# Gated linear attention feeding a SoLU block: the third token group's key work and scans placed before the second period

## The chip, the cores and the metric

The kernel runs on one core of a Trainium2 chip. The core has five engines that run side by side and wait for each other by semaphores: PE (matrix multiplication, with weight loads counted apart as PEld), DVE (VectorE), ACT (ScalarE), POOL (GpSimd) and SP (SyncE, which here only issues DMA transfers). Each engine works through its own instructions in the order in which the program gives them. The metric is the device time of one execution in microseconds (us).

## The reference

```python
# attention: batch 4, heads 8, sequence 768, head dimension 48, float32
state = np.zeros((B, H, D, D))
for t in range(S):
    state = alpha[:, :, t, :, None] * state + einsum('bhd,bhe->bhde', k[:, :, t], v[:, :, t])
    y[:, :, t] = einsum('bhd,bhde->bhe', q[:, :, t], state)
x = y.transpose(0, 2, 1, 3).reshape(B * S, H * D)      # 3072 tokens x 384

# SoLU block: w_in 384 x 1024, w_out 1024 x 384
h = x @ w_in
e = exp(h - max(h)); solu = h * e / sum(e)
ln = (solu - mean(solu)) / sqrt(var(solu) + 1e-06) * g_ln
out = ln @ w_out
```

## The kernel before, in words

**Tiling.** The 768 positions are cut into G = 6 groups of 128. A group holds the 128 positions of all four batches, 512 tokens, and is taken through two stages: attention (which makes `x`, 384 features by 512 tokens) and the SoLU block. In the SoLU block the 1024 hidden features are eight slices of 128. `up(g, f)` multiplies one slice (L366, six matmuls recorded for each, because float32 counts twice), takes its exponential on ACT (`e`, L380), the product h*e on DVE (`room`, L381) and its square on ACT (`u2`, L382). `running(g, f)` adds e on POOL and u2 on DVE into running sums (L397). `e` and `u2` have three buffers each, `h` has two PSUM banks. `down(n, half)` multiplies by w_out for one batch of a group (L477), and `finish(n)` scales and stores it (L495 to L511).

**Attention of a group.** The decay products over a group are made by scans on DVE. The steps, by the names that the plans use:

- `alpha` (alpha_T, L192, made for the group after the one in hand): alpha is transposed on DVE into `aT` and its range is checked on ACT (alpha_over, L197); then the alpha of one group further is loaded over it.
- `back` (scan_back, L211): three backward scans on DVE, `aT` to `hT`.
- `keys` (keys_T, L227, and keys, L231): the keys `kn` are transposed on DVE into `kT` (one transpose of 128x1024, one of 128x512), POOL multiplies them by `hT`, and the next group's keys are loaded over `kn`.
- `on2`, `on0`, `on1` (scan_on, L216): three forward scans on DVE, in place on `aT`; the one for part 2 first copies `fend` (L220). Each begins with `least` (L223) and a reciprocal (L224).
- `lasts`, `firsts`: the queries `qn` are transposed on DVE into `qe` and `qv`, and POOL multiplies them by `aT` (queries, L241); after `firsts` the next group's queries are loaded.
- `apart` (L235): ACT spreads `qe` over two parts of `qv`.
- `decay` (L246): POOL multiplies the state by the group's total decay.
- `keys_back` (L284): PE turns `kT` back, ACT copies the result to `kg`.
- `scores0`, `scores1` (L262): PE multiplies keys and queries for four heads at a time into four PSUM banks (a0 to a3); `masked0`, `masked1` (L276): DVE multiplies by the causal mask into `sT`. Both halves use the same four banks, and so do `keys_back`, the outputs y and the state update.
- `read0` to `read3` (L315): PE reads the old state into y. `values` (read_values, L323, then next_state, L333): PE adds sT times v to y, ACT copies y to `x` (L331), and PE makes the state update `kv`, which DVE adds to the state (L351).

**Order.** The schedule is written out by hand: the order of the calls is the order on every engine. Groups 0 and 1 have their attention in a straight-line part (L622 to L783), together with loading and unpacking the weights and all downs of group 0. Behind that comes the loop at L858, one *period* for each g = 1 to 5. Period g runs the eight ups of group g, the downs of group g - 1 (none in period 1, whose list `todo` is empty) and the attention of group g + 1 (up to g = 4). A plan says at which of the eight steps s each part of that attention comes: `head` before up(g, s), `behind` after it, `middle` after the running sums, and `tail` after the down of the step. Period 1 has the plan `first`, period 2 the plan `second`, later periods `usual`. Under `first` the backward scans of the next group (`back`) are not made; `second` makes them late, as `back_late` at its step 0.

**SP's queue.** All loads in the loop and the stores of finish (but for the last group) are issued by SP, in program order: a store waits for its scaled output on ACT, `load_v` for the state update that still reads the old v, loads of k and q for the DVE transposes of the old ones, a load of alpha for alpha_over.

Of the kernel before, what the change touches and what calls it, by code (L numbers as in the profile page):

```python
# [32 lines left out]
def fast_path(ctx, tc, q, k, v, alpha, moe_w_in, moe_w_out, moe_g_ln, out):  # L33
# [68 lines left out]
    kn = const.tile([P, H, TQ, D], FP, name="kn")  # L102
# [26 lines left out]
    def load(src, dst, g):  # L129
        t = slice(g * P, (g + 1) * P)  # L130
        for b in range(B):
            nc.sync.dma_start(
                out=dst[32 * b : 32 * b + 32].rearrange("t h u d -> t h (u d)"),
                in_=src[b, :, t, :].rearrange("h (t u) d -> t h (u d)", u=TQ),
            )
# [47 lines left out]
    def firsts(src, dst):  # L183
        nc.vector.transpose(out=dst.rearrange("p h (t u) -> p h u t", u=TQ), in_=src[:, :, :, 0:E0])  # L184

    def lasts(src, dst):
        nc.vector.transpose(
            out=dst.rearrange("p j (i t u) -> p u j i t", u=TQ, i=2),
            in_=src[:, :, :, E0:D].rearrange("p (j i) u d -> p u j i d", i=2),
        )  # L190

    def alpha_T(g):  # L192
        nc.gpsimd.memset(aT[:, :, 0:1], 0.0)
        firsts(an, aT[:, 0:H, 1:SW])
        lasts(an, aT[:, H:NB, 1:SW])
# [9 lines left out]
    def scan(out, data, start, flip):  # L205
        a, o, s = (x.rearrange("p j s -> p (j s)") for x in (data, out, start))
        if flip:
            a, o, s = a[:, ::-1], o[:, ::-1], s[:, ::-1]
        nc.vector.tensor_tensor_scan(out=o, data0=a, data1=s, initial=1.0, op0=ALU.mult, op1=ALU.add)  # L209

    def scan_back(g, i):  # L211

        part = slice(NP * i, NP * i + NP)
        scan(h4[:, part], aT[:, part], unit, True)

    def scan_on(g, i):  # L216
        part = slice(NP * i, NP * i + NP)
        s = seed[i % 2]
        if i == 2:
            nc.vector.tensor_copy(out=fend[:, g], in_=h4[:, :, 1])  # L220

        least = small.tile([P, NP, 1], FP, name="least")
        nc.vector.tensor_scalar(out=least, in0=h4[:, part, 1:2], scalar1=LEAST, scalar2=None, op0=ALU.max)  # L223
        nc.vector.reciprocal(out=s[:, :, 0:1], in_=least)  # L224
        scan(aT[:, part], aT[:, part], s, False)

    def keys_T(g):  # L227
        firsts(kn, kT[:, 0:H])
        lasts(kn, kT[:, H:NB])

    def keys(g):  # L231
        for part in (slice(0, H), slice(H, NB)):
            nc.gpsimd.tensor_tensor(out=kT[:, part], in0=kT[:, part], in1=hk[:, part], op=ALU.mult)  # L233
# [64 lines left out]
    def y_mm(b, a, r, row, lhsT, rhs, stop=False):  # L298
        begun = reading["begun"]
        nc.tensor.matmul(  # L300
            y_bank(b)[quarter(r), a], lhsT=lhsT, rhs=rhs, start=(b, r) not in begun, stop=stop,
            tile_position=(row, 32 * r), skip_group_check=True,
        )
        begun.add((b, r))
# [18 lines left out]
    def read_values(g, batches=range(B)):  # L323
        if 0 in batches:
            gr[g]["x"] = pair.tile([P, KC, B, P], FP, name="x")
        for b in batches:
            for n, (a, hs) in enumerate(parts):
                for r, (h, e) in enumerate(hs):
                    y_mm(b, a, r, 0, vn[:, b, h, e], sT[:, b, h], n == len(parts) - 1)
        for b in batches:  # L330
            nc.scalar.copy(out=gr[g]["x"][:, :, b], in_=reading["y"][b])  # L331

    def next_state(g):  # L333
        kv = banks("kv", [H, 64], 2)
        for j in range(NB):
            for b in range(B):
                if j < H:
                    o, e = kv[0][quarter(b), j], vn[:, b, j, 0:64]
                else:
                    i = 2 * (j - H)  # L340
                    o, e = kv[1][quarter(b), i : i + 2], vn[:, b, i : i + 2, 0:64]
                nc.tensor.matmul(  # L342
                    o, lhsT=kg[:, j, quarter(b)], rhs=e, start=True, stop=True, tile_position=(0, 32 * b),
                    skip_group_check=True,
                )
        for i in range(2):
            s = state[:, H * i : H * i + H, 0:64]
            if g == 0:
                nc.scalar.copy(out=s, in_=kv[i])
            else:  # L350
                nc.vector.tensor_tensor(out=s, in0=s, in1=kv[i], op=ALU.add)  # L351
# [426 lines left out]
    load(alpha, an, 3)  # L778
    for i in range(3):
        scan_back(2, i)  # L780
    read_values(1)
    next_state(1)
    finish(3)  # L783
# [3 lines left out]
    usual = dict(  # L787
        head={4: "keys_back", 5: "masked0", 6: "masked1"},
        behind={0: "v keys", 1: "on2 on0 on1", 2: "lasts firsts", 3: "apart", 5: "decay", 6: "alpha", 7: "back"},
        tail={4: "scores0", 5: "scores1", 6: "begin read0 read1", 7: "values"},  # L790
        middle={7: "read2 read3"},
    )
    first = dict(
        head={4: "keys_back", 6: "masked0", 7: "masked1"},
        behind={0: "v keys", 1: "on2 on0", 2: "on1 lasts", 3: "firsts", 4: "apart", 5: "decay", 7: "alpha"},
        tail={5: "scores0", 6: "scores1", 7: "begin read0 read1 read2 read3 values"},
        middle={},
    )
    second = dict(
        head={4: "keys_back", 6: "masked0", 7: "masked1"},  # L800
        behind={0: "back_late", 1: "v keys", 2: "on2 on0 on1", 3: "lasts firsts", 4: "apart", 5: "decay", 6: "alpha", 7: "back"},
        tail={5: "scores0", 6: "scores1", 7: "read2 read3 values"},
        middle={7: "begin read0 read1"},
    )

    def attend(a, what):

        more = a + 1 < G
        if what == "v":
            load_v(a)  # L810
        elif what == "keys":
            keys_T(a)
            keys(a)
            if more:
                load(k, kn, a + 1)
        elif what[:2] == "on":
            scan_on(a, int(what[2]))
        elif what == "lasts":
            lasts(qn, qe)
            queries(2)  # L820
        elif what == "firsts":
            firsts(qn, qv[:, 0:H])
            queries(0)
            queries(1)
            if more:
                load(q, qn, a + 1)
        elif what == "apart":
            apart()
        elif what == "decay":
            decay(a)  # L830
        elif what == "keys_back":
            keys_back(a)
        elif what[:6] == "scores":
            scores(a, int(what[6]))
        elif what[:6] == "masked":
            masked(int(what[6]))
        elif what == "alpha" and more:
            alpha_T(a + 1)
            alpha_over(a + 1)
            if a + 2 < G:  # L840
                load(alpha, an, a + 2)
        elif what == "back" and more:
            for i in range(3):
                scan_back(a + 1, i)
        elif what == "back_late":
            for i in range(3):
                scan_back(a, i)
        elif what == "begin":
            read_begin()
        elif what[:4] == "read":  # L850
            read_state(int(what[4]))
        elif what == "values":
            read_values(a)
            next_state(a)
# [2 lines left out]
    todo = []  # L857
    for g in range(1, G + 1):  # L858
        rise, att = g < G, g + 1 < G
        plan = {1: first, 2: second}.get(g, usual)  # L860

        def at(where, s):
            for what in plan[where].get(s, "").split() if att else ():
                attend(g + 1, what)

        after = None
        if not rise:
            break
        for s in range(FC):
            at("head", s)  # L870
            if rise:
                up(g, s)
            if after is not None:
                finish(after)
                after = None
            if s == 0 and g > 1:
                token_sums(g - 1)
            at("behind", s)
            for f in centres.get(s, ()) if g == 1 else ():
                centre(f)  # L880
            if rise and s:
                running(g, s)
            at("middle", s)
            if todo:
                n, half = todo.pop(0)
                down(n, half)
                if half:
                    after = n
            at("tail", s)
        if after is not None:  # L890
            finish(after)
        todo = [(n, half) for n in range(g * B, g * B + B) for half in range(2)]
# [493 lines left out]
```

## Time and profile before

| | |
|---|---|
| median of 14 runs | 405.13 us (401.61 to 408.27) |
| the profiled execution | 406.92 us; span of its core 405.1 us |
| mean granted clock of PE | 0.985 |
| busy: PE, DVE, ACT, POOL | 378.5, 255.8, 146.2, 117.6 us |
| up matmuls L366 | 288, 592 ns median of one |
| down matmuls L477 | 384, 491 ns mean of one |
| DVE backward scans L209, each | 1257 ns mean |
| DVE forward scans L209, each | 1387 ns mean |
| POOL key products L233 | 8, 1739 ns mean |
| first up matmul of periods 1 to 5, start | 117.97, 162.15, 220.81, 278.28, 335.75 us |
| k load, one of four issues of a group | 192 KB, 4.2 us to landing |

The profile is of one execution. The rows of the group table give, for one line of the program and one engine, the number of instructions, their busy time and the mean of one, and the time that the engine stood idle just before them with what ended it. In a timeline a row is one instruction, or a merged stretch of the same instruction ("x12"), with its start from the beginning of the span. "issue" as the cause of a pause means that the profile shows nothing that was waited for. The stretches between the starts in the table's row of the first up matmuls are the periods.

### The profile page before, as it was taken

The page shows a single profiled execution, that of the slowest core. Times are in us where ns is not written, and L with a number is a line of the kernel's source. Part 1 is how long each engine was busy: PE and PEld are TensorE (multiplying, and loading weights), DVE is VectorE, ACT ScalarE, POOL GpSimd, SP SyncE. Part 2 cuts the span into 40 slices and gives each one's busy share as a digit, 9 for nine tenths or more (in the row PEclk, how much of TensorE's full clock was granted, in tenths as well). Part 3 has the DMA queues.
Part 4 walks back from the last instruction along what each step waited for, and adds up shares of the span by engine and source line. Part 5 has one row for each costly group of instructions (what it writes and reads, how often), then busy time and mean ns, then how long its engine had stood idle before and what let it go on. Part 6 is the DMA issues. An engine that isn't in the chain of part 4 may idle for free. (4 is left out here: it accounts for less than half of the span.)

```text
span 405.1 us, 11119 instructions
## 1 busy us (share of the span) xinstructions
PE 378.5 (93%) x4929; PEld 229.4 (57%) x4929; DVE 255.8 (63%) x415; ACT 146.2 (36%) x253; POOL 117.6 (29%) x118
## 2 busy tenths in 40 slices
PE   8686999788988898999999999999999999999995
PEld 8673436356664357555557555567555675555552
DVE  1978789994929874699592795574875413444410
ACT  3535575553332525123351224243152122222100
POOL 5010000030005696074630438120466110333200
PEclk9998999998999899999999999999999999999999
DMA  9956969403319203632130833002400000000111
GB/s 186 196 159 171 227 196 194 97 19 80 79 48 170 60 22 83 79 98 47 52 100 4 134 69 92 2 23 41 59 19 21 23 3 21 15 15 11 40 40 47
DMA packets 86409, 30.82 MB, mean 76 GB/s; under 512 B 67912, under 2 KB 84560, under 8 KB 86352
## 3 DMA queue, kind: packets, MB, share of 16 engines
q1 hardware_dynamic: 85328, 29.11, 33.2%
q8 instruction: 40, 0.66, 0.7%
q10 hardware_dynamic: 1024, 0.92, 0.7%
q14 instruction: 17, 0.14, 0.1%
HBM read 25.30 MB, written 4.72 MB: 74 GB/s over the span
## 5 line engine op out<-in xcount | busy, mean ns | idle before, releaser
L366 PE MATMUL h<-x,w_in 128*128 128x512 f32 x288 | 135.4, 612 | 6.9 <-DVE g_col L596 4.2
L477 PE MATMUL o<-w_out,room 128*128 128x385 f32 x384 | 133.2, 491 | 1.1 <-DVE least L223 1.1
L477 PEld LDWEIGHTS o<-w_out,room 128*128 128x128 f32 x384 | 71.4, 190 | 57.2 <-issue 15.4
L366 PEld LDWEIGHTS h<-x,w_in 128*128 128x128 f32 x288 | 53.5, 192 | 67.6 <-issue 50.8
L381 DVE TENSOR_TENSOR room<-h,e 128x512 f32<-128x512 f32 x40 | 27.6, 690 | 56.7 <-ACT e L380 56.6
L508 POOL TENSOR_TENSOR r<-sums,mhalf 128x1 f32<-128x1 f32 x20 | 12.1, 607 | 172.2 <-DVE sums L500 172.1
L380 ACT ACTIVATE e<-h 128x512 f32<-128x512 f32 x40 | 23.9, 596 | 82.2 <-PE h L366 82.2
L397 POOL TENSOR_TENSOR p<-p,e 128x512 f32<-128x512 f32 x30 | 42.1, 1403 | 21.9 <-ACT e L380 21.7
L382 ACT ACTIVATE u<-room 128x512 f32<-128x512 f32 x40 | 25.2, 630 | 50.1 <-DVE room L381 50.1
L279 DVE TENSOR_TENSOR sT<-a,mask 128x512 f32<-128x512 f32 x44 | 27.3, 682 | 12.4 <-PE a L268 12.4
L268 PE MATMUL a<-qv,kT 32*128 32x128 f32 x704 | 26.2, 291 | 4.5 <-DVE qv L758 2.0
L268 PEld LDWEIGHTS a<-qv,kT 32*128 32x128 f32 x704 | 23.2, 197 | 11.5 <-issue 3.6
L397 DVE TENSOR_TENSOR p<-p,u 128x512 f32<-128x512 f32 x30 | 24.0, 800 | 7.0 <-ACT u L382 7.0
L209 DVE TENSOR_TENSOR_SCAN hT<-aT,unit 128x516 f32<-128x516 f32 x18 | 21.8, 1257 | 8.2 <-ACT aT L655 8.2
L209 DVE TENSOR_TENSOR_SCAN aT<-aT,seed 128x516 f32<-128x516 f32 x18 | 25.0, 1387 | 0.6
L351 DVE TENSOR_TENSOR state<-state,kv 128x512 f32<-128x512 f32 x10 | 6.9, 688 | 28.7 <-PE kv L342 28.7
L300 PE MATMUL y<-sT,vn 128*32 128x128 f32 x768 | 22.9, 274 | 1.4 <-issue 0.8
L331 ACT COPY x<-y 128x384 f32<-128x384 f32 x24 | 11.5, 479 | 31.6 <-PE y L300 31.6
L233 POOL TENSOR_TENSOR kT<-kT,hT 128x1024 f32<-128x1024 f32 (+1 forms) x8 | 13.7, 1739 | 31.5 <-DVE kT L184 31.5
L300 PEld LDWEIGHTS y<-sT,vn 128*32 128x32 f32 x768 | 20.8, 110 | 3.7 <-issue 2.8
L300 PE MATMUL y<-qv,state 32*32 32x128 f32 x1280 | 20.1, 278 | 2.0 <-issue 1.6
L300 PEld LDWEIGHTS y<-qv,state 32*32 32x32 f32 x1280 | 15.9, 103 | 9.5 <-issue 6.5
(140 smaller groups left out, 388.2 us busy)
## 6 DMA issues: line engine op xcount, KB each, us to landing
an<-in_alpha_dram SPq DMA_DIRECT2D x20, 192.0 KB, 4.2
out_dram<-o_sb SPq DMA_DIRECT2D x20, 192.0 KB, 1.9
room<-in_moe_w_out_dram SPq DMA_DIRECT2D x8, 384.0 KB, 3.7
kn<-in_k_dram SPq DMA_DIRECT2D x16, 192.0 KB, 4.2
qn<-in_q_dram SPq DMA_DIRECT2D x16, 192.0 KB, 3.5
vn<-in_v_dram SPq DMA_DIRECT2D x5, 512.0 KB, 5.7
room<-in_moe_w_in_dram SPq DMA_DIRECT2D x16, 128.0 KB, 4.0
kn<-in_k_dram SPq DMA_DIRECT2D x4, 384.0 KB, 5.8
```

The lines of the kernel that those rows point to most:

```text
L209: nc.vector.tensor_tensor_scan(out=o, data0=a, data1=s, initial=1.0, op0=ALU.mult, op1=ALU.add)
L233: nc.gpsimd.tensor_tensor(out=kT[:, part], in0=kT[:, part], in1=hk[:, part], op=ALU.mult)
L268: nc.tensor.matmul(a[b][:, i], lhsT=kT[quarter(b), kb], rhs=qv[quarter(b), qb], start=kb == h, stop=kb != h, tile_position=(32 * b, 0), sk ...
L279: nc.vector.tensor_tensor(out=sT[:, b, half * NP : half * NP + NP], in0=a[b], in1=mask[:, None, :].to_broadcast([P, NP, P]), op=ALU.mult,)
L300: nc.tensor.matmul(y_bank(b)[quarter(r), a], lhsT=lhsT, rhs=rhs, start=(b, r) not in begun, stop=stop, tile_position=(row, 32 * r), skip_g ...
L366: nc.tensor.matmul(h, lhsT=w_in[:, a, f * P : (f + 1) * P], rhs=d["x"][:, a].rearrange("p b t -> p (b t)"), start=(a == 0), stop=(a == KC ...
L380: nc.scalar.activation(out=e, in_=h, func=AF.Exp)
L381: nc.vector.tensor_tensor(out=u, in0=h, in1=e, op=ALU.mult)
L382: nc.scalar.activation(out=u2, in_=u, func=AF.Square)
L397: eng.tensor_tensor(out=p, in0=d[0][i] if f == 1 else p, in1=d[f][i], op=ALU.add)
L477: nc.tensor.matmul(d["o"][:, 0 : DM + 1], lhsT=u_of(g, f)[:, b * P : b * P + P], rhs=w_out[:, f], start=(f == 0), stop=(f == FC - 1), skip ...
L508: nc.gpsimd.tensor_tensor(out=r, in0=s[:, 3:4], in1=mhalf, op=ALU.pow)
```

## The change

In the straight-line part, after the backward scans of group 2, the keys of group 2 are transposed and multiplied, the load of group 3's keys is issued, and two of the three forward scans of group 2 are made. All this now comes ahead of `read_values(1)`, `next_state(1)` and `finish(3)` in program order. Period 1's plan loses these parts. Its remaining parts come a step earlier at several places, its state reads are split between steps 6 and 7, and it makes the backward scans of group 3 at step 7. The plan `second` and the late backward scans are taken out; period 2 runs under `usual`.

```diff
     load(alpha, an, 3)
     for i in range(3):
         scan_back(2, i)
+    keys_T(2)
+    keys(2)
+    load(k, kn, 3)
+    scan_on(2, 2)
+    scan_on(2, 0)
     read_values(1)
     next_state(1)
     finish(3)
...
     first = dict(
-        head={4: "keys_back", 6: "masked0", 7: "masked1"},
-        behind={0: "v keys", 1: "on2 on0", 2: "on1 lasts", 3: "firsts", 4: "apart", 5: "decay", 7: "alpha"},
-        tail={5: "scores0", 6: "scores1", 7: "begin read0 read1 read2 read3 values"},
-        middle={},
-    )
-    second = dict(
-        head={4: "keys_back", 6: "masked0", 7: "masked1"},
-        behind={0: "back_late", 1: "v keys", 2: "on2 on0 on1", 3: "lasts firsts", 4: "apart", 5: "decay", 6: "alpha", 7: "back"},
-        tail={5: "scores0", 6: "scores1", 7: "read2 read3 values"},
-        middle={7: "begin read0 read1"},
+        head={3: "keys_back", 5: "masked0", 6: "masked1"},
+        behind={0: "v", 1: "on1", 2: "lasts firsts", 3: "apart", 5: "decay", 7: "alpha back"},
+        tail={4: "scores0", 5: "scores1", 6: "begin read0 read1", 7: "values"},
+        middle={7: "read2 read3"},
     )
...
-        elif what == "back_late":
-            for i in range(3):
-                scan_back(a, i)
...
-        plan = {1: first, 2: second}.get(g, usual)
+        plan = first if g == 1 else usual
```

For comparison, the plan `usual`, which is not changed:

```python
head={4: "keys_back", 5: "masked0", 6: "masked1"},
behind={0: "v keys", 1: "on2 on0 on1", 2: "lasts firsts", 3: "apart", 5: "decay", 6: "alpha", 7: "back"},
tail={4: "scores0", 5: "scores1", 6: "begin read0 read1", 7: "values"},
middle={7: "read2 read3"},
```

## The prediction

> **What bounds the kernel now.** I read the page's busy shares first (PE 93%), then the chain that ended last (the last 0.8 us only, no use), then busy time by stretch. The stretches run from the first up matmul (L366) of one period to that of the next: "period g" is the pass of the L858 loop with that g. The columns after the length are busy time and count for PE, PEld, DVE, ACT, POOL, then the granted clock and the DMA share.
>
> ```profile
> core 0: us, PE busy (x) PEld busy (x) DVE busy (x) ACT busy (x) POOL busy (x), PEclk, DMA share, GB/s
> 110.70:117.20 6.50, 4.77 (x194) 4.35 (x190) 0.03 (x1) 1.92 (x4) 0.00 (x0) 1.00 0.33 79
> 118.00:162.10 44.10, 39.12 (x671) 23.76 (x668) 33.33 (x45) 17.81 (x30) 28.67 (x25) 0.96 0.39 78
> 162.10:220.80 58.70, 58.30 (x768) 35.04 (x764) 43.27 (x61) 19.15 (x32) 21.41 (x19) 1.00 0.31 66
> 220.80:278.30 57.50, 57.50 (x769) 34.54 (x765) 37.87 (x60) 19.94 (x33) 20.96 (x20) 1.00 0.28 57
> ```
>
> Period 3 (last row) already runs under the later plan and PE never pauses: 57.5 us is its own work. Period 2 does the same work in 58.7, so at most 1.2 us is to be had there. Period 1 is the loose one: it has no down matmuls, so its own work is 57.5 less period 3's eight downs (2.6 to 2.8 us each in PE's timeline, 21.3 together) and the token sums (0.6): 35.6 us. It takes 44.2. The other 8.6 us are waits and a slow clock. In the first row DVE and POOL stand still for 6.5 us just before it, while PE reads out group 1.
>
> Who holds PE in period 1: the waits there, then DVE's and PE's timelines (start, duration, instruction, idle before it).
>
> ```profile
> ACT u L382 <- DVE room L381: 13.7, 8, 5.7
> PEld h L366 <- DVE room L381: 4.4, 3, 2.9
> ```
> ```profile
> 117.22 0.69 DVE L351 TENSOR_TENSOR state<-state,kv 128x512 f32<-128x512 f32 x1 [6.49 <-PE kv L342]
> ...
> 122.09 2.04 DVE L184 STREAM_TRANSPOSE kT<-kn 128x1024 f32<-128x1024 f32 x1
> 123.97 1.10 DVE L187 STREAM_TRANSPOSE kT<-kn 128x512 f32<-128x512 f32 x1
> ...
> 125.50 0.99 DVE L220 COPY fend<-hT 128x12 f32<-128x12 f32 x1
> ...
> 126.81 1.88 DVE L209 TENSOR_TENSOR_SCAN aT<-aT,seed 128x516 f32<-128x516 f32 x1
> 128.61 1.18 DVE L223 TENSOR_SCALAR least<-hT 128x4 f32<-128x4 f32 x1
> ...
> 130.04 1.23 DVE L209 TENSOR_TENSOR_SCAN aT<-aT,seed 128x516 f32<-128x516 f32 x1
> ...
> 131.77 0.68 DVE L381 TENSOR_TENSOR room<-h,e 128x512 f32<-128x512 f32 x1
> ```
> ```profile
> 132.51 4.97 PE L366 MATMUL h<-x,w_in 128*128 128x512 f32 x7 [2.66 <-DVE room L381]
> ```
>
> The room product that frees an h bank (there are two) sits behind fend, two scans and a running sum, from 125.50 to 131.77, so PE stands for 2.66 us. The 0.99 us fend and 1.18 us least are small operations (0.16 each elsewhere) that ran late because POOL's key product and running sum lay beside them.
>
> **The change, ahead of period 1.** Moved to DVE after scan_back(2), which ends at 110.7: the key transposes (starts 122.09 to 124.90: 2.8 us), fend, least, reciprocal and scan for part 2 (125.50 to 128.61: 3.1, with POOL's delay in it), the same for part 0 (1.5; the second least's delay came from a running sum that isn't there). 7.4 us in a gap of 6.5. Place by place: transposes to 113.5; POOL's products 112.9 to 116.1 (their row: 3.3); fend to 115.1; scan 2 to 117.3; scan 0 to 118.8. Queued behind on DVE are the two state additions (were 117.22, now 118.75) and finish(3), each 1.3 us late. Nobody needs the new state before POOL's decay, 20 us on; kv's banks are next wanted by keys_back near 126. finish(3)'s ACT scaling delays the first exponential from 120.85 to 121.75, its room product from 121.5 to 122.4, and PE needs that only for up 2 at 123.1. Cost 0; without PE's two h banks it would be the 0.9.
> The k load of group 3 (four issues, 3.1 us on SP) now follows alpha's at about 113.6 and precedes finish(3)'s store and the v load, which wait for later things anyway; the v load moves by 0.9 us, and is wanted 25 us on. The q load goes 7 us earlier.
>
> **Period 1**, with the rows' durations, absolute times as before. DVE: room 1 at 124.3; scan 1 waits for POOL's first running sum (124.3 to 125.6) and ends 127.2; running 1; room 2 at 127.7 (it was 131.77); q transposes 128.3 to 131.3; running 2; room 3 at 131.7. PE: up 2 to 125.75, keys_back (1.3) to 127.05, up 3 to 129.6, up 4 to 132.2. No wait on room is left. What is late next is scores0: POOL's q products end 134.3, and apart on ACT, which comes after keys_back's copies (1.5), e3 and u2 3, ends at 134.35. PE waits 132.2 to 134.5: **2.3**. Scores0 to 136.5, masks 138.1 to 140.5 (running 4 holds DVE while POOL runs), up 5 has ended at 139.1: wait **1.45** before scores1, since both halves use the same four banks and no down stands between them. Then masks1 against read0: **0.4**. At the end ACT's alpha_over (3.35 from 152.1) delays the copies of y, whose banks kv needs: **0.8**. Sum 4.95 + 35.6 = 40.5 against 44.2: **-3.7**.
> The clock has to be added.
>
> ```profile
> 130.20:133.60 3.40, 1.09 (x3) 0.62 (x4) 3.33 (x6) 1.11 (x2) 0.00 (x0) 1.00 0.21 39
> 133.60:137.00 3.40, 3.40 (x6) 1.35 (x5) 3.40 (x5) 0.86 (x3) 1.92 (x2) 0.53 0.01 2
> ...
> 154.10:157.50 3.40, 1.84 (x84) 1.37 (x68) 2.12 (x3) 2.49 (x4) 3.40 (x4) 1.00 0.02 5
> ```
>
> A stretch of 3.4 us in which PE worked 1.09 is followed by one at half clock; one in which it worked 1.84 isn't. My 2.3 us wait leaves 1.1 if it falls in one such stretch, and more if it straddles two. At half clock the scores take 3.61 (the row at 92.61) and not 2.0, right on the path: 0 to **+1.6**. It lies at the edge, so I take +0.8.
> [...]
>
> **Period 2** gets the plan of period 3 (masks one step earlier, reads apart) and loses the three late scans at its start (3.5 us of DVE). It begins with the same state as period 3, the state additions about a microsecond later and the next room product another microsecond behind them: 57.5, **-1.2**. If the additions were later still, token_sums would hold PE; I bound that at +0.5.
>
> Sum: -3.7 + 0.8 - 1.2 = **-4.1**. The profiled execution took 406.92 (span 405.1), so 402.8 there. It is 1.8 above the median of the runs; from the median, 405.13 - 4.1 = **401.0**.
>
> **Rivals.**
> *Denser than I think.* POOL and DVE get in each other's way less, apart comes in time, and period 1 keeps only waits of about 0.8: 36.4, so -7.8 - 1.2 = -9.0: 396.1; halfway there, with only the 2.3 us wait shortened to 0.5 and no slow clock, -6.7: 398.4. For it: DVE has 7 us less work in this period. Against: scores now follow up 4 with no step in between, where before PE still waited at 139.7 and 140.8 with a step more.
> *The wait only moves.* The 2.3 us become 4 (q products behind running sums on POOL) and the clock drops fully: -4.1 + 1.7 + 0.8 = -1.6: 403.5, hardly to be told from no change. For it: POOL has the same 28.7 us less 3.3 in a shorter period, and apart must wait for both POOL and ACT.
> *Slower: the k load in front of PE's densest code.* PE already pauses for nothing that the profile shows, twice just there:
>
> ```profile
> 112.13 2.93 PE L300 MATMUL y<-sT,vn 128*32 128x128 f32 x99 [0.82 <-issue]
> ...
> 116.41 1.63 PE L342 MATMUL kv<-vn,kg 128*32 128x64 f32 x70 [0.90 <-issue]
> 158.00:160.00 2.00, 2.00 (x82) 2.00 (x75) 0.00 (x0) 1.21 (x3) 0.19 (x1) 1.00 0.80 200
> ```
>
> [...] If each pause grew to a k transfer's landing (4.2 us by the DMA table), it would cost 3.4 + 3.3 = 6.7, net +2.6: 407.7. It decides from 2.9 us a pause. Against: the last row, the same matmuls at DMA share 0.80 without a pause, and a 1.56 us pause at 156.31 with share 0.02.
> [...]
>
> **Chances.** Forecast (399.3 to 403.1) 0.52; denser 0.22; the wait only moves 0.18; slower 0.08. 0.5% is 2.0 us, about what a measurement can tell, so faster means under 403.1: 0.52 + 0.22 + 0.02 = 0.76; same 0.16; slower 0.08. The range runs from the middle of the denser case, 397, to just past the moved wait, 404.5.
>
> **What would show it.** Right: key transposes and two scans between 110.7 and 119, DVE idle there near zero; no wait of L366 on room over 1 us; period 1 near 40 to 42 us, with waits before both scores; period 2 at 57.5; pauses at 111 to 117 still under 1 us each. Wrong: period 1 starting over 1 us later (prelude step), a wait before scores0 over 4 us, or period 2 over 58.5.

## The result and the profile after

The changed kernel took 397.13 us (median of 10 runs, 396.46 to 402.1) against 404.83 us before (median of 47 runs, 401.61 to 408.49). The ratio of its runs to those of before is 0.9852, with a 95% interval of 0.9814 to 0.9889: about 6 us less, between 4.5 and 7.5. The ratio goes by the means of those runs that lie within 1.5% of the fastest of their kernel (here 398.65 us against 404.65, without five of the 47; in the experiments a run of 487 us of the kernel before and one of 966 us of the last version fall out by this too). The medians lie further apart, by 7.7 us, because the changed kernel's runs fall into two clumps, six at 396.5 to 397.2 us and four at 400.8 to 402.1: the median stands in the lower one, the mean between them. The profiled execution took 398.24 us (span 396.4).

Busy time by stretch of the changed kernel; columns as before: length, busy time of PE, PEld, DVE, ACT and POOL, granted clock, DMA share.

```profile
108.22:116.32 8.10, 6.72 (x212) 5.38 (x203) 7.96 (x10) 1.92 (x4) 3.35 (x2) 1.00 0.66 157
114.90:154.50 39.60, 38.34 (x671) 23.08 (x668) 30.63 (x41) 17.39 (x30) 24.08 (x23) 1.00 0.33 61
154.50:212.00 57.50, 57.50 (x769) 34.53 (x765) 38.72 (x60) 19.37 (x32) 20.39 (x19) 1.00 0.37 75
```

The first row is DVE's work that was put ahead of period 1; the gap of 6.5 us in which DVE did nothing is gone. Period 1 (second row) takes 39.6 us and not 44.2, with the clock at full speed throughout. Period 2 (third row) takes 57.5 and not 58.7; PE never pauses in it.

Who holds PE in period 1 now (all of PE's rows in the waits of that stretch), and PE's timeline at those places:

```profile
PE a L268 <- POOL qv L244: 0.4, 1, 0.4
PE a L268 <- ACT qv L237: 0.3, 1, 0.3
PE h L366 <- DVE room L381: 0.3, 1, 0.3
```
```profile
120.58 2.84 PE L366 MATMUL h<-x,w_in 128*128 128x512 f32 x6 [0.27 <-DVE room L381]
...
130.32 0.50 PE L268 MATMUL a<-qv,kT 32*128 32x128 f32 x8 [0.43 <-POOL qv L244]
131.15 2.01 PE L268 MATMUL a<-qv,kT 32*128 32x128 f32 x56 [0.33 <-ACT qv L237]
133.09 2.84 PE L366 MATMUL h<-x,w_in 128*128 128x512 f32 x6
135.86 3.62 PE L268 MATMUL a<-qv,kT 32*128 32x128 f32 x64
```

The 2.66 us wait for room is down to 0.27. The last row is a nearly hidden wait: 64 score matmuls take 2.07 us elsewhere and 3.62 here, because they stop between the first ones until the masks of the first half have freed the banks. No wait of PE's rows shows these 1.55 us; the whole list has 0.6 of them, at the weight loads (PEld).

DVE ahead of period 1:

```profile
108.22 2.06 DVE L184 STREAM_TRANSPOSE kT<-kn 128x1024 f32<-128x1024 f32 x1
110.09 1.25 DVE L187 STREAM_TRANSPOSE kT<-kn 128x512 f32<-128x512 f32 x1
111.08 1.57 DVE L220 COPY fend<-hT 128x12 f32<-128x12 f32 x1
...
112.98 1.88 DVE L209 TENSOR_TENSOR_SCAN aT<-aT,seed 128x516 f32<-128x516 f32 x1
...
115.17 1.23 DVE L209 TENSOR_TENSOR_SCAN aT<-aT,seed 128x516 f32<-128x516 f32 x1
116.32 1.26 DVE L351 TENSOR_TENSOR state<-state,kv 128x512 f32<-128x512 f32 x2
```

8.1 us from the first transpose to the state additions, which now follow without a gap; fend (1.57) and the first scan (1.88) lie beside POOL's key product (110.43 to 113.78) and again take longer than elsewhere (0.16 and 1.23).

### The profile page after: what moved, and what is told of

Its sections match the earlier page's. It is cut to its first block, busy times and chain, and to the rows that moved or that the text cites. A ratio compares the mean times of both kernels' runs of the same rounds, so it can differ in the third digit from the quotient of the medians.

```text
span 396.4 us, 11123 instructions
## 1 busy us (share of the span) xinstructions
PE 375.2 (95%) x4929; PEld 227.4 (57%) x4929; DVE 254.5 (64%) x415; ACT 146.1 (37%) x253; POOL 115.4 (29%) x118
## 5 line engine op out<-in xcount | busy, mean ns | idle before, releaser
L397 POOL TENSOR_TENSOR p<-p,e 128x512 f32<-128x512 f32 x30 | 41.0, 1365 | 24.7 <-ACT e L380 24.4
L397 DVE TENSOR_TENSOR p<-p,u 128x512 f32<-128x512 f32 x30 | 24.8, 827 | 8.6 <-ACT u L382 8.6
L268 PE MATMUL a<-qv,kT 32*128 32x128 f32 x704 | 25.0, 278 | 4.6 <-DVE qv L758 2.0
L268 PEld LDWEIGHTS a<-qv,kT 32*128 32x128 f32 x704 | 22.0, 186 | 11.8 <-DVE qv L758 2.8
L300 PE MATMUL y<-sT,vn 128*32 128x128 f32 x768 | 23.1, 274 | 1.3 <-issue 0.8
L300 PEld LDWEIGHTS y<-sT,vn 128*32 128x32 f32 x768 | 20.8, 110 | 4.2 <-issue 2.7
L300 PEld LDWEIGHTS y<-qv,state 32*32 32x32 f32 x1280 | 15.3, 103 | 7.6 <-issue 4.1
L300 PE MATMUL y<-qv,state 32*32 32x128 f32 x1280 | 19.0, 278 | 0.0
L201 ACT ACTIVATE sq<-an,mone 128x1536 uint8<-128x1536 f32 x12 | 18.8, 1570 | 0.2
```

Of the source, the lines that this page charges most:

```text
L201: nc.scalar.activation(out=sq, in_=x, func=AF.Relu, scale=sign, bias=mone, accum_out=over[:, g, i : i + 1])
L268: nc.tensor.matmul(a[b][:, i], lhsT=kT[quarter(b), kb], rhs=qv[quarter(b), qb], start=kb == h, stop=kb != h, tile_position=(32 * b, 0), sk ...
L300: nc.tensor.matmul(y_bank(b)[quarter(r), a], lhsT=lhsT, rhs=rhs, start=(b, r) not in begun, stop=stop, tile_position=(row, 32 * r), skip_g ...
L397: eng.tensor_tensor(out=p, in0=d[0][i] if f == 1 else p, in1=d[f][i], op=ALU.add)
```

## The experiments

The table gives, for each kernel, the length of periods 1 and 2 and of a *stretch* from the first state read of group 1 (the first 32x32 matmul of L300 after the scores of group 1) to the first up of period 3, all from one profiled execution. The stretch starts behind the half-clock stretches of the straight-line part; the two pauses at issue ahead of period 1 lie in it and still differ (1.2 to 2.0 us together without fillers). Times are medians; a ratio is to the kernel before on the same chip, with its 95% interval. The chips differ between the rows, so their times are compared by the ratios.

| kernel | period 1 | period 2 | stretch | time | ratio |
|---|---|---|---|---|---|
| before | 44.18 | 58.66 | 117.04 | 404.83 | |
| changed | 39.62 | 57.47 | 110.95 | 397.13 | 0.985 (0.981 to 0.989) |
| only the move | 39.17 | 58.87 | 112.19 | 400.35 | 0.990 (0.985 to 0.995) |
| only the plans | 44.73 | 57.47 | 116.48 | 402.17 | 0.998 (0.993 to 1.003) |
| old period 2 | 39.24 | 58.77 | 111.92 | 400.37 | 0.989 (0.983 to 0.996) |
| k load in period 1 | 39.09 | 57.48 | 110.59 | 399.32 | 0.986 (0.979 to 0.993) |
| keys alone ahead | 43.02 | 57.48 | 114.79 | 401.75 | 0.994 (0.990 to 0.998) |
| three scans ahead | 40.43 | 57.47 | 111.94 | 398.17 | 0.987 (0.982 to 0.992) |
| one filler | 39.71 | 57.48 | 111.27 | 400.22 | 0.990 (0.986 to 0.994) |
| two fillers | 42.59 | 57.73 | 113.41 | 400.71 | 0.990 (0.986 to 0.994) |
| before, two fillers | 47.03 | 60.04 | 119.92 | 407.66 | 1.007 (1.003 to 1.011) |
| second scores later | 43.47 | 57.48 | 114.66 | 401.69 | 0.994 (0.990 to 0.998) |
| two fillers, output banks | 40.58 | 57.50 | 111.21 | 399.21 | 0.987 (0.982 to 0.993) |
| output banks | 38.04 | 57.48 | 109.95 | 396.09 | 0.976 (0.970 to 0.983) |

### The move without the new steps, and the new steps without the move

```diff
-        head={3: "keys_back", 5: "masked0", 6: "masked1"},
-        behind={0: "v", 1: "on1", 2: "lasts firsts", 3: "apart", 5: "decay", 7: "alpha back"},
-        tail={4: "scores0", 5: "scores1", 6: "begin read0 read1", 7: "values"},
-        middle={7: "read2 read3"},
+        head={4: "keys_back", 6: "masked0", 7: "masked1"},
+        behind={0: "v", 2: "on1 lasts", 3: "firsts", 4: "apart", 5: "decay", 7: "alpha"},
+        tail={5: "scores0", 6: "scores1", 7: "begin read0 read1 read2 read3 values"},
+        middle={},
...
+    second = dict(...)      # as before, with back_late
```

> Only the move ahead of period 1: the period keeps the old steps for what is left in it, and period 2 its old plan with the late scans. Theory (the waits of up matmuls on room came from the key chain on DVE, and the move alone takes them away): no wait of L366 on room over 1 us, period 1 at 39 to 41 us against 44.2 before and 39.6 after the change, period 2 at 58.5 to 59; time 4 to 5 us under before. Rival (the earlier steps of the plan are what shortens period 1): period 1 at 42 to 44, time within 2 us of before.

PE in period 1 of this kernel has no wait for room, neither at up 2 nor at up 4:

```profile
118.40 10.57 PE L366 MATMUL h<-x,w_in 128*128 128x512 f32 x24
...
130.11 5.32 PE L366 MATMUL h<-x,w_in 128*128 128x512 f32 x12
```

Period 1 took 39.17 us and period 2 58.87, and the time is 4.0 us under before by the ratio: as the theory had it. The move alone does all that the change does for period 1.

```diff
-    keys_T(2)
-    keys(2)
-    load(k, kn, 3)
-    scan_on(2, 2)
-    scan_on(2, 0)
...
-        behind={0: "v", 1: "on1", ...},
+        behind={0: "v keys", 1: "on2 on0 on1", ...},
```

> Only the new steps: keys and both scans stay in period 1 (steps 0 and 1), the other parts stand at the steps of the changed kernel, period 2 runs under the later plan. Theory (the move matters): keys_back now also waits for POOL's key product, rooms stay late, period 1 at 43 to 46 us, period 2 at 57.5; time 0 to 2 us under before. Rival (the steps matter): period 1 at 41 or less, time 4 us or more under before.

Period 1 44.73, period 2 57.47. The rows of PE in this kernel, and the stretch of its period 1:

```profile
127.18 1.80 PE L287 MATMUL tp<-ident,kT 128*128 128x128 f32 x12 [0.55 <-POOL kT L233]
...
134.72 5.49 PE L366 MATMUL h<-x,w_in 128*128 128x512 f32 x6 [3.15 <-DVE room L381]
```
```profile
118.60:163.40 44.80, 40.61 (x674) 23.47 (x669) 36.31 (x47) 17.54 (x30) 28.29 (x25) 0.92 0.34 63
```

keys_back now waits for POOL, the room wait is back at 3.15 us, and the up behind it takes 5.49 us in place of 2.74, at half clock (0.50 from 133.9 to 140.7 us; 0.92 is the mean over the period). The rival that the steps shorten period 1 has fallen.

### Period 2's plan

```diff
-        behind={..., 5: "decay", 7: "alpha back"},
+        behind={..., 5: "decay", 7: "alpha"},
...
+    second = dict(...)      # as before, with back_late
-        plan = first if g == 1 else usual
+        plan = {1: first, 2: second}.get(g, usual)
```

> The changed kernel, but the backward scans of the fourth group are made late in period 2, under period 2's old plan. Theory: period 1 as after the change or up to 0.5 us shorter (39.1 to 39.6), period 2 at 58.5 to 59, time 1 us above the changed kernel. Rival (period 2 was shortened by what the new period 1 hands over, not by its plan): period 2 at 57.5.

Period 1 39.24, period 2 58.77, the stretch 1.0 us longer than the changed kernel's. Period 2's gain hangs on its plan (1.3 us here). The 0.4 us by which period 1 is shorter are not the price of the backward scans that the new plan puts into it: they lie ahead of keys_back, which begins 8.36 us after the first up in the changed kernel, with the 0.27 us wait for room, and 7.99 here. The next kernel has these scans in period 1 too and takes 39.09. The time is 0.4% above the changed kernel by the ratios, with overlapping intervals, so the 1 us rests on the stretch.

### The place of the k load

```diff
     keys(2)
-    load(k, kn, 3)
...
-        behind={0: "v", ...},
+        behind={0: "v kload", ...},      # kload: load(k, kn, 3)
```

> The changed kernel, but the load of the fourth group's keys stays in period 1, behind the v load. Theory (the load's place is worth nothing): both pauses at issue in the values and state matmuls ahead of period 1 stay at 0.6 to 0.9 us, period 1 at 39.6, time as the changed kernel within 1 us. Rival (the load disturbs PE's code there): the pauses fall below 0.3 us each and the time falls by 1 us.

The 6 us around PE's value and state matmuls, first with the load left in period 1, then in the changed kernel:

```profile
112.00:118.00 6.00, 5.00 (x199) 4.65 (x198) 5.86 (x9) 1.92 (x4) 3.35 (x2) 1.00 0.29 73
```
```profile
109.00:115.00 6.00, 5.04 (x199) 4.69 (x198) 5.90 (x8) 1.92 (x4) 3.35 (x2) 1.00 0.67 169
```

DMA share 0.29 against 0.67, PE busy 5.00 against 5.04 us for the same 199 matmuls. The pauses at issue are 0.91 and 0.63 us without the load and 0.76 and 0.63 with it. Period 1 took 39.09, 0.5 us less than expected, because PE arrived later and no up waits for room. The stretch is 0.4 us shorter and the ratio 0.986 against 0.985: the load's place is worth nothing that these runs can tell. The load does not lengthen the pauses, and with that the slower rival of the prediction falls.

### Less ahead, and more

```diff
-    scan_on(2, 2)
-    scan_on(2, 0)
...
-        behind={0: "v", 1: "on1", ...},
+        behind={0: "v", 1: "on2 on0 on1", ...},
```

> The changed kernel with only the keys ahead and all three forward scans at step 1 of period 1. Theory (DVE's order in front of room 2 is what held PE, and the scans are the larger part of it): room 2 comes some 3 us later than after the change, PE waits about 2 us for it at up 4, period 1 at 41.5 to 43 us; time 2 to 3 us above the changed kernel. Rival (the keys alone were the chain, with POOL's product): period 1 within 0.7 us of 39.6.

```profile
129.23 2.84 PE L366 MATMUL h<-x,w_in 128*128 128x512 f32 x6 [1.43 <-DVE room L381]
133.77 0.50 PE L268 MATMUL a<-qv,kT 32*128 32x128 f32 x8 [1.70 <-POOL qv L244]
```

PE waits 1.43 us for room (about 2 was expected) and then 1.70 us for POOL's query product, and a half-clock stretch follows that costs about 1.6 us (the scores take 3.03 in place of 2.01, the up behind them 3.43 in place of 2.84). Period 1 is 43.02, just over the 43 that was expected, and the time 0.9% (3.7 us) above the changed kernel by the ratios. The two scans are worth 3.4 us of period 1, with that half-clock stretch in it.

```diff
     scan_on(2, 0)
+    scan_on(2, 1)
...
-        behind={0: "v", 1: "on1", 2: ...},
+        behind={0: "v", 2: ...},
```

> The changed kernel with all three forward scans ahead of period 1. Theory (the DVE work ahead has slack: nobody waits soon for the state additions and finish behind it): DVE's additions 1.4 us later, first room product of period 1 some 0.5 to 1.5 us later, up 2 waits for it 0.3 to 1.5 us more, and the query chain comes 1.4 us earlier; period 1 between 39 and 40 us, time within 1 us of the changed kernel. Rival (the gap was just filled, and every us more is paid): period 1 at 41 us or more.

40.43 us, 0.4 above what was expected: up 2 now waits 2.02 us for room.

```profile
116.64 1.26 DVE L351 TENSOR_TENSOR state<-state,kv 128x512 f32<-128x512 f32 x2
...
120.15 0.69 DVE L381 TENSOR_TENSOR room<-h,e 128x512 f32<-128x512 f32 x1 [1.27 <-ACT e L380]
```

DVE's additions begin 3.2 us after the first up (113.45), and the first room product follows 3.5 us behind them through finish(3), POOL's power and ACT's scaling. Over the kernels the wait of up 2 goes with this lag: 0.89 us (k load in period 1) and 1.01 (output banks) no wait, 1.42 (changed) 0.27, 2.89 (two fillers) 1.73, 3.19 here 2.02. Some 1.15 us are free, and all beyond is paid in full. The change uses this slack up when PE reaches period 1 early.

### The scatter

The half-clock stretches of the profiled executions are not at the same places: apart from one at the very end (from 403.5 us in the kernel before, 394.2 in the changed one), they start in the kernel before at 34.8, 92.9 and 133.8 us (granted clock 0.50 for 3.4 us), in the changed kernel only at 32.4; the kernel with the k load in period 1 has one at 34.9, and its first scores of group 1, from 92.77, take 3.65 us where the changed kernel's take 2.06. The one at 92.9 follows a wait of 2.02 us before the scores of group 1. The granted clock of a run goes with its time: of twelve executions of the changed kernel, two more than those of the median, the four over 400 us have 0.985 to 0.988, the eight others 0.993 to 0.998. By estimate, 3.4 us at half clock lower the mean of 395 us by 0.0043 and cost 1.7 us, so the 0.009 between the means of the two groups stand for two such stretches, or 3.5 us; the groups' times lie 4.2 us apart. One filler keeps PE busy in the wait before the scores; its results are not used.

```diff
     down(2, 0)
+    warm(12, ps_h, "h")
     scores(1, 0)
```

> The changed kernel with 12 idle matmuls (1.9 us of PE, results unused) in the 2 us wait before the scores of group 1. Theory (half-clock stretches of 3.4 us, which come or not from run to run, make the scatter; one of them follows this wait): no stretch under full clock between 88 and 100 us, first scores in 2.1 us and not 3.6, the start of period 1 unmoved otherwise; the runs near 401 us become rarer or fall by 1.7 us. Rival (the scatter comes from elsewhere, and the filler only delays the scores): granted clock as in the other kernels, time 0 to 1 us above the changed kernel.

PE's rows from 88 to 100 us show no half clock, the first scores take 2.07 us, and the runs keep within 399.3 to 401.3; but the median is 3 us above the changed kernel, not 0 to 1 (1.9 us by the ratios): the runs near 397 us are gone, not those near 401. Its profiled execution has two half-clock stretches in a row at 32.4 to 39.2, which the filler does not touch, and a pause at issue of 1.68 us ahead of period 1. Two fillers were put against that, in both kernels:

```diff
     keys_back(0)
+    warm(13)
     in_range(0)
...
     down(2, 0)
+    warm(12, ps_h, "h")
     scores(1, 0)
```

> The changed kernel with idle matmuls in two waits of the straight-line part: 13 before the first up of group 0 (a wait of 3 to 4 us), 12 before the scores of group 1. Theory (the half-clock stretches behind these two waits, 1.7 us each and one to three of them per execution, make most of the scatter): no stretch under full clock after 30 us except at the very end, scatter of the runs under 2.5 us, median 0 to 2 us under the changed kernel. Rival: scatter of 4 us or more as in the changed kernel.

> The kernel before with the same idle matmuls in the same two places. Theory: its only half-clock stretch left is the one in period 1 behind the wait for room, so against the changed kernel with the same matmuls it is longer by periods 1 and 2 alone, 102.8 less 97.1 = 5.7 us (4.5 to 6.5). Rival (the change also shifts the straight-line part, or the scatter): a difference under 4 or over 7 us.

The scatter shrinks to 2.3 us (399.65 to 401.93) and 3.4 us, and from 25 to 225 us no half-clock stretch is left in either profile (the first scores of group 1 take 2.07 us in both). That holds for period 1 of the kernel before too, where one was expected behind the wait for room: the wait is there (2.67 us), the clock stays at 1.00. But neither kernel became faster (0 to 2 us were expected). The kernel before has a ratio of 1.007 to itself without fillers; the changed kernel has 0.990 in place of 0.985, with overlapping intervals. The medians, 400.71 and 407.66, are 7.0 apart and the stretches 6.5, at the upper edge of the 4.5 to 6.5 that were expected or above it, and hardly short of the rival's 7. PE in the kernel before with two fillers:

```profile
151.97 0.97 PE L300 MATMUL y<-qv,state 32*32 32x128 f32 x54 [1.90 <-issue]
152.88 2.37 PE L300 MATMUL y<-sT,vn 128*32 128x128 f32 x74
155.70 1.62 PE L300 MATMUL y<-sT,vn 128*32 128x128 f32 x51 [0.45 <-issue]
157.06 0.28 PE L342 MATMUL kv<-vn,kg 128*32 128x64 f32 x2
157.12 0.31 PE L300 MATMUL y<-sT,vn 128*32 128x128 f32 x3
157.17 1.40 PE L342 MATMUL kv<-vn,kg 128*32 128x64 f32 x72
160.25 0.86 PE L342 MATMUL kv<-vn,kg 128*32 128x128 f32 x22 [1.68 <-issue]
```

From pause to pause there are 54 + 74 = 128 matmuls, then 51 + 2 + 3 + 72 = 128. Without fillers the first pause of period 1 came after 252 reads, here after 202: the 25 matmuls of the fillers left 50 records. So in these two executions the pauses went by a count of PE's matmuls, and the added ones moved them, into three places of period 1 that cost 4.03 us (1.90, 0.45 and 1.68) in place of 1.56. In the changed kernel with two fillers the stretch is 2.5 us longer than without them: the pauses in it sum to 2.40 us in place of 1.39, and up 2 waits 1.73 us for room in place of 0.27, because PE reaches period 1 early. The fillers' gain at the clock is given back there.

### A faster period 1

The largest wait left is that of the second scores. First they were put behind up 6:

```diff
-        head={3: "keys_back", 5: "masked0", 6: "masked1"},
-        behind={..., 5: "decay", 7: "alpha back"},
-        tail={4: "scores0", 5: "scores1", 6: "begin read0 read1", 7: "values"},
-        middle={7: "read2 read3"},
+        head={3: "keys_back", 5: "masked0", 7: "masked1"},
+        behind={..., 5: "decay", 6: "scores1 alpha", 7: "back"},
+        tail={4: "scores0", 7: "read2 read3 values"},
+        middle={7: "begin read0 read1"},
```

> The changed kernel with period 1's second scores behind up 6, its masks behind them under up 7, the four state reads after up 7, and alpha a step earlier. Theory (after the change the largest wait left in period 1 is that of the second scores on the first masks, 1.5 us): that wait goes, period 1 at 38 to 38.5 us, unless the four reads in one piece bring back the 1.56 us pause at issue (then 39.6); time 0 to 1.5 us under the changed kernel. Rival (PE is held by DVE's or POOL's total in this period): the wait turns up in front of the reads, period 1 at 39.6 or more.

43.47 us, as the rival had it: the scores ran in 2.07 us, but the wait turned up in front of the reads, 1.58 and twice 0.20 us for the masks. That is 0.4 us more than the 1.55 us that were saved; the other loss is that the reads, in one piece, paused for 1.10 and 1.56 us at issue.

Then the second scores were given other banks. In period 1 the two output banks are idle; the masks of batches 2 and 3, whose banks are still shared, come first.

```diff
-        head={3: "keys_back", 5: "masked0", 6: "masked1"},
+        head={3: "keys_back", 5: "swapped0", 6: "swapped1"},   # masked(i, (2, 3, 0, 1))
...
-        tail={4: "scores0", 5: "scores1", ...},
+        tail={4: "scores0", 5: "scores_o", ...},               # scores(a, 1, [o, o, a2, a3])
```

> The changed kernel with the idle matmuls in the two waits, and in period 1 and later the masks of batches 2 and 3 ahead of 0 and 1 in period 1's plan, whose second scores go to the two output banks (idle in this period) for batches 0 and 1. Theory (the second scores wait 1.5 us for four masks because they share their banks): they wait at most 0.4 us, period 1 at 38.0 to 38.5 us, 1 to 1.5 us under the kernel with idle matmuls alone. Rival (the wait moves to the reads or to the end of the period): period 1 at 39.3 or more.

With two fillers the second scores took 2.35 us (135.80 to 138.15; 3.54 from start to start without the other banks) and the median fell by 1.5 us to 399.21, as expected. But of the 2.0 us by which period 1 became shorter only 1.2 are the scores; its pauses at issue, too, came to 0.30 us in place of 1.40. Period 1 was 40.58 and not under 38.5, since up 2 waited 1.74 us for room at its start: PE came early and DVE's additions lagged by 2.89 us.

> The changed kernel with period 1's second scores in the output banks for batches 0 and 1 and the masks of batches 2 and 3 first, without the idle matmuls, so that PE's instruction count, and with it the places of the pauses at issue, is that of the changed kernel. Theory: the second scores take 2.1 to 2.5 us and not 3.6; from the first state read of group 1 to the first up of period 3 it takes 109.5 to 110.5 us (changed kernel 110.95, before 117.04); ratio to before 0.979 to 0.984, 1 to 1.5 us under the changed kernel. Rival (the 1.3 us come back as a wait for room, alpha_over or the copies): 110.9 or more, time as the changed kernel.

Without fillers, stretches of periods 1 and 2:

```profile
113.80:151.80 38.00, 36.90 (x671) 22.36 (x668) 30.05 (x39) 17.40 (x30) 24.14 (x23) 1.00 0.33 61
151.80:209.30 57.50, 57.50 (x768) 34.51 (x764) 38.65 (x60) 19.37 (x32) 20.39 (x19) 1.00 0.38 75
```

Period 1 is 38.04 us, the stretch 109.95, 1.0 us under the changed kernel, and the median 396.09 us. The second scores take 2.35 us again. The ratio, 0.976, is lower than the 0.979 to 0.984 that were expected. The kernel is ahead of both others by its medians; against the changed kernel the intervals of the ratios overlap, so that margin rests on the trace.

## Why the prediction was right, and where it was off

**Direction and mechanism: right.** The gain was to come from DVE's gap ahead of period 1, through the room waits; undoing the move brought the room wait back (3.15 us) and period 1 to 44.73, and the move alone gave 39.17. The profiled kernel before had a half-clock stretch in period 1 and the changed one none, so the gain there could have been chance of the clock. It was not: the kernel before with two fillers has none there either, and its period 1, less the 2.47 us by which its pauses at issue grew, takes 44.56 us.

**The prelude step (cost 0): right here, but thinner than it was told.** The DVE chain was worked out at 8.05 us and took 8.1. The additions came 1.42 us behind the first up, where 0.78 was worked out, and 0.27 us was paid. The slack behind the step is about 1.15 us, and the version with three scans ahead paid the rest.

**Period 1: -3.7 and +0.8 for the clock, measured -4.56 and no half-clock stretch.** Several terms were mis-sized. The wait before scores0 was put at 2.3 us and was 0.76 (0.43 and 0.33). The chain through POOL and apart was worked out well (the scores go on 16.25 us after the first up, 16.5 was worked out). But PE got to the scores 0.8 us later than worked out, and the first eight score matmuls, which need only POOL's first product, ran inside the wait. The clock stayed at 1.00 around this wait, so the clock term of 0.8 became 0. The other way, PE's own work was put at 35.6 us, by taking the downs off period 3; it is 39.62 less the waits of 0.27, 0.76, 1.55 and 0.29, that is 36.75. The 1.15 us between them lie in the eight ups (21.73 in this period, 21.2 in period 3), in the first scores, which the waits cut in two (2.44 against 2.0), and in the values (3.70 against 3.52). The wait before the second scores was right (1.45, measured 1.55); the one at the reads (0.4) was nothing; the one at the end (0.8) was 0.29.

**Period 2: -1.2, measured -1.19.** The experiment with its old plan gives it back, 58.77.

**Sum: -4.1, measured -5.75 in periods 1 and 2 and -6.09 over the stretch.** That agrees with the ratio (about -6); the 0.34 between the two are the pauses at issue ahead of period 1. So the sum was a third too small. The forecast of 401.0 had 399.3 to 403.1 around it: the median, 397.13, lies below that and only 0.13 us above the end of the range, and the ratio, taken from 405.13, gives 399.1, just below it as well. That the median fell into the lower of two clumps is chance. The profiled executions differ by 8.7 us because the later one also reached period 1 3.1 us earlier, in code that the change does not touch: it had no half-clock stretch at its scores of group 1 (1.6 us: the first scores took 2.06 and not 3.61), and its first up started at 32.73 and not 33.75. This share is chance of the execution; in the kernel with the k load in period 1 the same scores take 3.65 us. What the medians' 7.7 us have over 6 is the two clumps of the changed kernel's runs, which the granted clock of each run tells apart; where the half-clock stretches of a run lie is shown only for the one execution that is profiled.

**The clock behind waits.** In the kernel before, the clock halved after a wait of 2.02 us (at 92.9) and after 2.66 (at 133.8). In other executions it stayed up after the same waits: 2.02 us in the changed kernel, 2.67 in the kernel before with two fillers. For the wait in question it made no difference: around its 0.76 us the clock stayed at 1.00, so the 0.8 was wrong by the size of the wait.

**The rivals.** The denser case was nearest: 398.4 with the scores0 wait at 0.5 and no slow clock, which is what happened to these two terms. The wait that only moves fell with the 0.76. The slower case fell with the k load experiment: the pauses are there, but the load does not lengthen them (0.91 and 0.63 us without it, 0.76 and 0.63 with it). That a pause would grow to the 4.2 us of a load's landing was the author's assumption; no run shows it.

## What to carry to other kernels

Work that blocks a chain in a busy period can be put into an idle gap of its engine ahead of it, but the price is set by who queues behind it in that gap: measure how much later the next in line may come (here 1.15 us), and put no more there than that allows. When two uses share banks, look for a row that takes longer than its twins (3.62 against 2.07 us); the list of waits has little of such a wait (here 0.6 of 1.55 us). And read two executions for chance, and the granted clock of every run, before crediting a change: the runs of the changed kernel with a clock of 0.985 to 0.988 here took some 4 us longer than the others.

## What the hardware showed that was not expected

Where many small matmuls followed each other, PE's pauses at issue came 128 matmul records apart (99 + 2 + 3 + 24 in the kernel before and in the changed one, 54 + 74 and 51 + 2 + 3 + 72 in the kernel before with two fillers) and cost 0.30 to 1.90 us; in the two executions compared they do not grow with DMA share (0.76 us beside 0.67, 0.91 beside 0.29). What the pauses are is not shown: the profile has nothing that PE waited for there. The 50 matmul records added in idle waits at 30 and 90 us moved them: in a stretch from 100 us on the kernel before paused 5.37 us in place of 3.28, the changed kernel 2.40 in place of 1.39.

The half-clock stretches inside the span lasted 3.4 us (34.8 to 38.2 in the kernel before), or two of them followed each other (133.9 to 140.7 with only the plans), and in the kernel before they stand on a grid: the starts at 34.8, 92.9 and 133.8 us are 17 and 12 steps of 3.41 us apart. In its rows, 3.4 us stretches with 1.09 and 1.36 us of PE work were followed by one, and one with 1.84 wasn't. Where the grid fell in an execution mattered: the 2.02 us wait before the scores of group 1 left 1.38 us of PE work in one step of the kernel before, and the next step ran at half clock; in the changed kernel the same wait lay across two steps with 2.45 and 2.34 us of work, and the clock stayed at 1.00. But PE's busy time in a step does not sort all the rows. By estimate from PE's timeline, a step with 1.79 us was followed by half clock (only the plans, from 89.55 us; the first scores took 3.47 us in place of 2.06), one with 1.48 us wasn't (the kernel before with two fillers, from 126.62). What else counts stays open.
